# Pieces of expert weights: three buffers for loads and for halves, split two steps behind the load, sent back earlier in a step; two buffers for queries and keys

## The chip, the cores and the metric

The kernel runs on one core of one Trainium2 chip. The metric is device time in microseconds of one execution, lower is better. The core has a matrix engine (PE, with its weight loads as PEld), a vector engine (DVE), a scalar engine (ACT), a general engine (POOL) and a sequencer for transfers (SP); each takes its instructions strictly in the order of the program, and they meet through semaphores. Transfers run on 16 DMA engines that all queues share.

## The reference

Three stages follow each other, on 2304 tokens of 512 numbers, all in fp32:

```
attn   = softmax(mask_by_64_blocks(q @ k.T / 8)) @ v      4 batches, 8 heads, 576 tokens, 64 wide
x1     = softplus(attn_rows @ w_in) @ w_out               512 -> 2048 -> 512
logits = x1 @ w_gate + softplus(x1 @ w_noise) * noise     8 experts, the best two per token
out    = sum over the two: weight * (relu(x1 @ w1[e]) @ w2[e])     512 -> 1024 -> 512
```

The kernel keeps fp32 accuracy on a 16-bit matrix engine by splitting numbers into a high and a low f16 half, so that one product becomes three.

## The kernel before, in words

The attention is cut into 32 phases (a batch, a pair of heads, and tokens 0 to 255 or 256 to 575), and those into 80 units of 128 queries, 2 in an early phase and 3 in a late one. The main loop (line 605) takes one unit per iteration n: `stage_s` issues the products q·k of unit n, `stage_e` the row maximum (L248, DVE) and the exponentials (L252, L257, L258, ACT) of unit n-1, `stage_p` the scaling into two f16 halves (L280 ACT, L286 DVE) and a transposing DMA (L298) of unit n-2, `stage_v` and `stage_v4` the products with v (L321, L333). Between these stand quanta of the first feed-forward network (`mlp_quantum`; its products are the rows "l" of line 74, its elementwise work L364 to L375) and the router (L408 to L479). All of it shares PE, ACT, DVE and SP.

Three background jobs run beside the units. First `w_step` brings in the 32 pieces of `w_in` and `w_out` (`w_load` into a tile `wst`, `w_conv` through a tile `wt`). When all 32 are there, `e_step` works on the expert weights: 64 pieces of 128x1024 fp32. `e_load` (L495) fetches a piece into a tile `est`, `e_conv` splits it into the two halves of a tile `eh`, the high one on ACT (L508) and the low one on DVE (L514), and `e_store` (L519) writes both halves back to a scratch tensor `wsc` in DRAM. Loads and stores go through SP's queue, as do the transposes of L298, the router's transposes (L421) and the loads of q, k and v (L186 to L197). The tiles `wst` and `est` share one tag with `bwst` buffers (2), `wt` and `eh` another with `beh` buffers (2); `bqk` (3) is the number of buffers for the split q and k.

An `e_step` stands at the end of an iteration, 0.9 times per iteration on average, and does three things in turn: store the piece that was split last, split the piece that was loaded last, load the next. The split of a piece thus stands one step behind its load, and its store two steps behind.

When the loop has ended, the pools of the attention are closed, the rest of the feed-forward network and the router run, and the expert stage (class `Moe`, lines L829 to L922) reads `wsc` back in pieces of 2 MB. In the trace PE has no idle time there from about 700 us on.

The order in which instructions of one engine stand is not the order of the code: a scheduler goes through the program with priorities (`hipri` lifts some lines) and a model of when a buffer, an engine and a result are ready. The numbers of buffers therefore move instructions on every engine, also far from the lines that are changed.

Of the kernel before, what the change touches and what calls it, by code (L numbers as in the profile page):

```python
# [38 lines left out]
    return [sum(runs[:t % LANES]) + t // LANES for t in range(n)]  # L39


CFG = dict(wa=4, wb=12, rate=2.0, rate2=1.55, lag0=4, rt='rt', hq='s', xq='s', pr=3, wq='s', vq='s', rq='s', braw=2, clr=30, w0=1, w1=2, ra=4, rb=1, he=50, hpp=50, bP=2, bP16=3, bwst=2, beh=2, bpt=6, bqk=3, bxt=3, gr=4, lag=2, bA=1, bR=1, bvv=4, bxr=2, bxT=2, bvr=1, l2b=2, budget=3, espread=0.9, hp=50, elo='v', pmode=('av', 'av', 'av', 'av'), wp=24, eld='s', est='s', l1b=2, sb=3, cpy=1, x2q='p', tq='s')


SYNC = mybir.DependencyInfo(mybir.DependencyClass.Sync, mybir.DependencyReason.DATA)
# [4 lines left out]
def body(nc, tc, i, o, stop=9):  # L50
    ctx = ExitStack()
    with ctx:
        return _body(ctx, nc, tc, i, o, stop)


def _body(ctx, nc, tc, i, o, stop):
    q, k, v, w_in, w_out = i["q"], i["k"], i["v"], i["moe_w_in"], i["moe_w_out"]
# [78 lines left out]
    def w_load(n):  # L136
        st = p1.tile([128, 1024], I32, name="wst", tag="wst", bufs=int(CFG["bwst"]))
        if n < 16:
            ENG[CFG['wq']].dma_start(st.rearrange("p (c f) -> p c f", c=4), w_in32[:, :, 256 * n:256 * n + 256])
        else:  # L140
            ENG[CFG['wq']].dma_start(st, w_out32[128 * (n - 16):128 * (n - 15), :])
        wraw[n] = st

    def w_conv(n):
        wd = wraw.pop(n).rearrange("p (f two) -> p f two", two=2)
        lo, hi = wd[:, :, 0], wd[:, :, 1]
        t = p1.tile([128, 1024], I32, name="wt", tag="eh", bufs=int(CFG["beh"]))
        t = t[:, :512]
        nc.vector.tensor_scalar(t, hi, scalar1=M1, scalar2=3, op0=ALU.bitwise_and, op1=ALU.logical_shift_left)
        nc.vector.scalar_tensor_tensor(t, hi, SGN, t, op0=ALU.bitwise_and, op1=ALU.bitwise_or)  # L150
        nc.vector.scalar_tensor_tensor(t, lo, 29, t, op0=ALU.logical_shift_right, op1=ALU.bitwise_or)
        w = t.bitcast(F32)
        if n < 16:
            sl = slice(128 * n, 128 * n + 128)
            d0, d1, sc = win[:, 0, :, sl], win[:, 1, :, sl], 1024.0
            w = w.rearrange("p (c f) -> p c f", c=4)
        else:
            d0, d1, sc = wout[:, 0, n - 16, :], wout[:, 1, n - 16, :], 2048.0
        nc.scalar.activation(d0, w, AF.Copy, scale=sc)
        if n < CFG["wp"]:  # L160
            nc.scalar.activation(w, w, AF.Copy, scale=sc)
            nc.gpsimd.tensor_tensor(d1, w, d0, op=ALU.subtract)  # L162
        else:
            nc.vector.scalar_tensor_tensor(d1, w, sc, d0, op0=ALU.mult, op1=ALU.subtract)
# [3 lines left out]
    def xt(g):  # L168
        if g not in xts:
            xts[g] = pm.tile([128, 8, GT], F16, name=f"xt{g}", tag="xt", bufs=int(CFG["bxt"]))  # L170
        return xts[g]
# [68 lines left out]
    def stage_e(u):  # L240
        T, s = u["T"], u["s"]
        esc = 2.0 ** -15
        sm = p1.tile([128, 8], F32, name="sm", tag="sm", bufs=8)
        u["sm"] = sm
        P = p1.tile([128, 2, 512], F32, name="P", tag="P", bufs=int(CFG["bP"]))
        wd = (128 * (T + 1),) * 2 if T < 4 else (320, 256)
        for hd in range(2):
            nc.vector.tensor_reduce(out=sm[:, hd:hd + 1], in_=s[hd][:, :wd[hd]], axis=AX.X, op=ALU.max, negate=True)  # L248
        if T < 4:
            nc.vector.tensor_scalar_mul(sm[:, 2:4], sm[:, 0:2], esc)  # L250
            for hd in range(2):
                nc.scalar.activation(P[:, hd, :wd[0]], s[hd][:, :wd[0]], AF.Exp, scale=esc, bias=sm[:, 2 + hd:3 + hd], accum_out=sm[:, 4 + hd:5 + hd])  # L252
        else:
            P = P.rearrange("p a b -> p (a b)")
            nc.vector.tensor_scalar(sm[:, 2:3], sm[:, 0:1], scalar1=sm[:, 1:2], scalar2=esc, op0=ALU.min, op1=ALU.mult)
            nc.gpsimd.memset(P[:, 576:640], 0.0)
            nc.scalar.activation(P[:, 0:320], s[0][:, :320], AF.Exp, scale=esc, bias=sm[:, 2:3], accum_out=sm[:, 4:5])  # L257
            nc.scalar.activation(P[:, 320:576], s[1][:, :256], AF.Exp, scale=esc, bias=sm[:, 2:3], accum_out=sm[:, 5:6])  # L258
        u["P"] = P
# [81 lines left out]
    def hipri(n=None):  # L341
        n = int(CFG["hp"] if n is None else n)
        return tc.high_priority(offset=n) if n else ExitStack()
# [146 lines left out]
    est = {}  # L490

    def e_load(n):
        e, c = divmod(n, 8)
        st = p1.tile([128, 1024], F32, name="est", tag="wst", bufs=int(CFG["bwst"]))
        ENG[CFG["eld"]].dma_start(st, i["wexp"][e, :, 1024 * c:1024 * c + 1024])  # L495
        est[n] = st
# [20 lines left out]
    def e_store(n):  # L517
        e, c = divmod(n, 8)
        ENG[CFG["est"]].dma_start(wsc[e, :, 2048 * c:2048 * c + 2048], est.pop(n))  # L519
# [20 lines left out]
    cnt = dict(att=True, chain=False, wl=0, wc=0, el=0, ec=0, es=0, c1=0, p2=0, ready=0, routed=0)  # L540
# [34 lines left out]
    def w_step(n):  # L575
        for _ in range(n):
            if cnt["wc"] < 32:
                if cnt["wc"] < cnt["wl"]:
                    w_conv(cnt["wc"])
                    cnt["wc"] += 1  # L580
                if cnt["wl"] < 32:
                    w_load(cnt["wl"])
                    cnt["wl"] += 1

    def e_step():
        if cnt["wc"] < 32:
            return
        if cnt["es"] < cnt["ec"]:
            e_store(cnt["es"])
            cnt["es"] += 1  # L590
        if cnt["ec"] < cnt["el"]:
            e_conv(cnt["ec"])
            cnt["ec"] += 1
        if cnt["el"] < 64:
            e_load(cnt["el"])
            cnt["el"] += 1
# [8 lines left out]
    while n < NU + 6 or cnt["es"] < 64:  # L605
        if n < NU:
            u = units[n]
            if u["first"]:
                u["ph"]["pt"] = [p1.tile([128, 8, 256] if u["has4"] else [128, 4, 256], F16, name=f"pt{hd}", tag="pt", bufs=int(CFG["bpt"])) for hd in range(2)]
                if u["has4"]:  # L610
                    u["ph"]["pt4"] = p1.tile([128, 10, 128], F16, name="pt4", tag="pt4", bufs=2)
            if n == 0:
                load_pair(*porder[0])
                w_step(1)
                load_v(*porder[0])
                load_pair(*porder[1])
                conv_pair(*porder[0])
                load_v(*porder[1])
                lp, cpi = 2, 1
            stage_s(u)  # L620
        while cpi < lp and first_unit[porder[cpi]] <= n + 1:
            conv_pair(*porder[cpi])
            cpi += 1
            if cpi < lp:
                load_v(*porder[cpi])
        while lp < len(porder) and first_unit[porder[lp]] <= n + 6 and lp - cpi < int(CFG["braw"]):
            load_pair(*porder[lp])
            if lp == cpi:
                load_v(*porder[lp])
            lp += 1  # L630
        if 1 <= n < NU + 1:
            with hipri(CFG["he"]):
                stage_e(units[n - 1])
        w_step(int(0 if n < CFG['wa'] else CFG['w0'] if n < CFG['wb'] else CFG['w1']))
        credit = min(credit + CFG["rate" if n < 36 else "rate2"], 3)
        if credit >= 1:
            credit -= mlp_quantum() > 0
        if 2 <= n < NU + 2:
            with hipri(CFG["hpp"]):
                stage_p(units[n - 2])  # L640
        if credit >= 1:
            credit -= mlp_quantum() > 0
        if 4 <= n < NU + 4:
            u = units[n - 4]
            if u["last"]:
                stage_v(u["ph"])
        if 5 <= n < NU + 5:
            u = units[n - 5]
            if u["last"] and u["has4"]:
                stage_v4(u["ph"])  # L650
        while credit >= 1 and mlp_quantum():
            credit -= 1
        while cnt["ready"] < NG and need[cnt["ready"]] <= n:
            cnt["ready"] += 1
        if n >= CFG["clr"] and n % 2 == 0 and cleared < 19:
            clear(cleared)
            cleared += 1
        eacc += CFG["espread"]
        while eacc >= 1 and n > 12:
            e_step()  # L660
            eacc -= 1
        n += 1
# [358 lines left out]
```

## Time and profile before

| | us |
|---|---|
| median of 3 executions | 1109.68 |
| lowest and highest | 1108.88, 1110.16 |
| the profiled execution | 1112.65 |
| its span | 1110.7 |
| PE busy | 999.6 (90%) |
| DVE busy | 599.9 (54%) |
| ACT busy | 546.5 (49%) |

Shares over the whole span mix two stages with different limits: up to about 600 us PE, DVE, ACT and the DMA engines are all loaded, and after 700 us PE alone is. What a change before 600 us is worth is read from the stretches there.

### The profile page before, as it was taken

The page shows a single profiled execution, that of the slowest core. Times are in us where ns is not written, and L with a number is a line of the kernel's source. Part 1 is how long each engine was busy: PE and PEld are TensorE (multiplying, and loading weights), DVE is VectorE, ACT ScalarE, POOL GpSimd, SP SyncE. Part 2 cuts the span into 40 slices and gives each one's busy share as a digit, 9 for nine tenths or more (in the row PEclk, how much of TensorE's full clock was granted, in tenths as well). Part 3 has the DMA queues.
Part 4 walks back from the last instruction along what each step waited for, and adds up shares of the span by engine and source line. Part 5 has one row for each costly group of instructions (what it writes and reads, how often), then busy time and mean ns, then how long its engine had stood idle before and what let it go on. Part 6 is the DMA issues. An engine that isn't in the chain of part 4 may idle for free.

```text
span 1110.7 us, 24476 instructions
## 1 busy us (share of the span) xinstructions
PE 999.6 (90%) x9526; PEld 661.4 (60%) x9526; DVE 599.9 (54%) x1756; ACT 546.5 (49%) x1132; POOL 200.0 (18%) x188
## 2 busy tenths in 40 slices
PE   4676899878978888889889999999999999999996
PEld 2353455545555556456556667767767777777674
DVE  6999898676877778787756536212111121121120
ACT  6687667767868687887756531211111112111111
POOL 0334101010010000101003421322222222222111
PEclk9998899988998899998999999999999999999999
DMA  6865679999999899999997489746999448796442
GB/s 168 192 178 171 171 188 272 262 238 288 269 273 275 242 256 247 289 257 251 226 254 273 114 325 236 134 73 146 330 325 248 78 84 210 189 330 149 116 105 30
DMA packets 272518, 234.96 MB, mean 212 GB/s; under 512 B 180110, under 2 KB 217486, under 8 KB 272400
## 3 DMA queue, kind: packets, MB, share of 16 engines
q1 hardware_dynamic: 223872, 148.15, 54.8%
q0 software_dynamic: 14176, 38.17, 14.1%
q10 hardware_dynamic: 34352, 47.04, 13.0%
q8 instruction: 76, 1.25, 0.5%
q14 instruction: 42, 0.34, 0.1%
HBM read 251.60 MB, written 58.79 MB: 279 GB/s over the span
## 4 chain that ended last, share of the span: by engine, by line
PE 43%; DVE 3%; DMA 2%; ACT 1%; issue 1%; SPq 0%; POOL 0%; POOLq 0%; ACTq 0%; DVEq 0%
PE ph L74 19%; PE py L74 17%; PE l L74 6%; DMA est<-in_wexp_dram 1%; DVE eh L514 1%; DMA xT<-xw 0%; DMA out_dram<-ys,si 0%; SPq L298 0%; DVE G L372 0%; DVE P L286 0%; ACT A L367 0%; ACT A L364 0%; ACT eh L508 0%; ACT P L252 0%; ACT R L375 0%
## 5 line engine op out<-in xcount | busy, mean ns | idle before, releaser
L74 PE MATMUL l<-xt,win 128*128 128x256 f16 x1728 | 229.1, 289 | 13.4 <-ACT R L375 6.6
L74 PEld LDWEIGHTS <-W 128*128 128x128 f16 x3936 | 223.2, 98 | 10.4 <-issue 0.9
L902 DVE SCALAR_TENSOR_TENSOR HT<-ph,HT 128x512 f16<-128x512 f32 x78 | 53.9, 692 | 324.5 <-ACT HT L901 324.5
L74 PE MATMUL l<-wout,G 128*128 128x512 f16 x864 | 209.6, 389 | 14.0 <-POOL wout L162 5.0
L74 PE MATMUL ph<-xT,W 128*128 128x128 f16 x3744 | 215.4, 219 | 0.8 <-DVE HT L902 0.8
L74 PE MATMUL py<-W,HT 128*128 128x512 f16 x936 | 208.4, 379 | 0.8 <-ACT ys L920 0.8
L74 PEld LDWEIGHTS <-win 128*128 128x128 f16 x1728 | 171.3, 103 | 51.8 <-issue 11.7
L74 PEld LDWEIGHTS <-HT 128*128 128x128 f16 x936 | 90.0, 98 | 102.4 <-issue 1.1
L74 PEld LDWEIGHTS <-G 128*128 128x128 f16 x864 | 81.9, 99 | 106.4 <-issue 19.1
L901 ACT ACTIVATE HT<-ph 128x512 f16<-128x512 f32 x78 | 46.6, 597 | 162.5 <-PE ph L74 158.4
L920 ACT ACTIVATE ys<-py,sw 128x512 f32<-128x512 f32 x39 | 26.8, 687 | 181.3 <-PE py L74 166.7
L227 PE MATMUL s<-k,q 64*128 64x128 f16 (+3 forms) x384 | 65.7, 332 | 45.8 <-ACT P L252 33.7
L286 DVE SCALAR_TENSOR_TENSOR P<-P,sm,P 128x128 f16<-128x128 f32 (+4 forms) x144 | 87.0, 618 | 24.0 <-ACT P L280 23.7
L280 ACT ACTIVATE P<-P,sm 128x128 f16<-128x128 f32 (+4 forms) x144 | 81.2, 586 | 23.9 <-DMA pt<-P 13.0
L471 POOL DMA_INDIRECT xsc<-xw,rpos x36 | 42.1, 1169 | 281.6 <-DMA xsc<-xw,rpos 99.7
L514 DVE SCALAR_TENSOR_TENSOR eh<-est,eh 128x1024 f16<-128x1024 f32 x64 | 77.7, 1219 | 23.9 <-ACT eh L508 22.2
L921 POOL DMA_INDIRECT out_dram<-ys,si x39 | 61.6, 1580 | 158.5 <-ACT ys L920 147.3
L508 ACT ACTIVATE eh<-est 128x1024 f16<-128x1024 f32 x64 | 67.2, 1053 | 38.9 <-DMA est<-in_wexp_dram 38.7
L248 DVE TENSOR_REDUCE sm<-s 128x1 f32<-128x256 f32 (+2 forms) x160 | 74.2, 477 | 13.4 <-PE s L229 9.9
L252 ACT ACTIVATE P<-s,sm 128x128 f32<-128x128 f32 (+3 forms) x128 | 66.1, 520 | 21.4 <-DVE sm L250 10.7
L227 PEld LDWEIGHTS <-q 64*128 64x128 f16 x384 | 23.9, 100 | 78.7 <-issue 60.3
L375 ACT ACTIVATE R<-l 128x512 f32<-128x512 f32 x72 | 42.1, 592 | 41.4 <-PE l L74 30.3
(201 smaller groups left out, 1005.0 us busy)
## 6 DMA issues: line engine op xcount, KB each, us to landing
W<-wsc ACTq DMA_DIRECT2D x76, 2048.0 KB
est<-in_wexp_dram SPq DMA_DIRECT2D x64, 512.0 KB
wsc<-eh SPq DMA_DIRECT2D x64, 512.0 KB
wst<-in_moe_w_in_dram SPq DMA_DIRECT2D x16, 512.0 KB
wst<-in_moe_w_out_dram SPq DMA_DIRECT2D x16, 512.0 KB
W<-wsc POOLq DMA_DIRECT2D x4, 2048.0 KB
out_dram<-zero ACTq DMA_DIRECT2D x19, 256.0 KB
rk<-in_k_dram SPq DMA_DIRECT2D x16, 288.0 KB
```

The costliest lines, as they stand in the source:

```text
L74: x = nc.tensor.matmul(*args, **kw)
L227: nc.tensor.matmul(s[hd][:, :N], Q[hs, a, 128 * T - q0:128 * T - q0 + 128], K[hs, c, :N], start=n == 0, stop=False)
L248: nc.vector.tensor_reduce(out=sm[:, hd:hd + 1], in_=s[hd][:, :wd[hd]], axis=AX.X, op=ALU.max, negate=True)
L252: nc.scalar.activation(P[:, hd, :wd[0]], s[hd][:, :wd[0]], AF.Exp, scale=esc, bias=sm[:, 2 + hd:3 + hd], accum_out=sm[:, 4 + hd:5 + hd])
L280: nc.scalar.activation(v4[:, :, 0, :], pin, AF.Copy, scale=r)
L286: nc.vector.scalar_tensor_tensor(v4[:, :, 1, :], pin, r, v4[:, :, 0, :], op0=ALU.mult, op1=ALU.subtract)
L375: nc.scalar.activation(R[:, h], ps, AF.Copy, scale=2.0 ** -21)
L508: nc.scalar.activation(hh, sv, AF.Copy, scale=sc)
L514: nc.vector.scalar_tensor_tensor(hl, sv, sc, hh, op0=ALU.mult, op1=ALU.subtract)
L901: nc.scalar.activation(HT[:, hf, 0:4], ph, AF.Relu)
L902: self.lo = nc.vector.scalar_tensor_tensor(HT[:, hf, 4:8], ph, 0.0, HT[:, hf, 0:4], op0=ALU.max, op1=ALU.subtract)
L921: nc.gpsimd.indirect_dma_start(out=self.out, out_offset=bass.IndirectOffsetOnAxis(ap=si, axis=0), in_=ys, in_offset=None, bounds_check=NTO ...
```

## The change

Three numbers in `CFG` change: `bwst` 2 to 3, `beh` 2 to 3, `bqk` 3 to 2. In `e_step` the store goes, and the split is held back until two pieces are loaded beyond those split (or all 64 are loaded). The store moves into the main loop, behind `stage_e` of the next iteration.

```
-CFG = dict(... bwst=2, beh=2, bpt=6, bqk=3, ...)
+CFG = dict(... bwst=3, beh=3, bpt=6, bqk=2, ...)
     def e_step():
         if cnt["wc"] < 32:
             return
-        if cnt["es"] < cnt["ec"]:
-            e_store(cnt["es"])
-            cnt["es"] += 1
-        if cnt["ec"] < cnt["el"]:
+        if cnt["ec"] < cnt["el"] - 1 or cnt["ec"] < cnt["el"] == 64:
             e_conv(cnt["ec"])
             cnt["ec"] += 1
         if cnt["el"] < 64:
...
         if 1 <= n < NU + 1:
             with hipri(CFG["he"]):
                 stage_e(units[n - 1])
+        if cnt["es"] < cnt["ec"]:
+            e_store(cnt["es"])
+            cnt["es"] += 1
         w_step(...)
```

How this moves instructions is seen in the order of the built programs. On SP's queue, where the expert pieces begin, the kernel before has two loads, two transposes of probabilities and the first store; the third load comes behind six more entries:

```order
L495 DMA est<-in_wexp_dram 128x1024 x2
L421 DMA_TRANSPOSE xT_1829<-xw 128x8x128
L298 DMA_TRANSPOSE pt_1642<-P_1899 128x2x128
L298 DMA_TRANSPOSE pt_1643<-P_1903 128x2x128
L519 DMA wsc<-eh 128x2048
```

In the changed kernel a first load stands six entries above these, and two more here, so that three loads are out when the first store is issued:

```order
L495 DMA est<-in_wexp_dram 128x1024 x2
L186 DMA rq<-in_q_dram 128x256
L186 DMA rk<-in_k_dram 128x256
L195 DMA vr<-in_v_dram 128x2x128
L421 DMA_TRANSPOSE xT_1829<-xw 128x8x128
L421 DMA_TRANSPOSE xT_1889<-xw 128x8x128
L298 DMA_TRANSPOSE pt_1642<-P_1899 128x2x128
L298 DMA_TRANSPOSE pt_1643<-P_1903 128x2x128
L519 DMA wsc<-eh 128x2048
```

What moved: a third load stands ahead of the first store, and the first split is two loads behind.

The second place is ACT where the attention ends. Before, the last three scalings of probabilities (L280) have 11 splits of expert pieces (L508) behind them, of which the first two are here:

```order
L280 ACTIVATE P_7558<-P,sm 128x4x128
L280 ACTIVATE P_7562<-P,sm 128x4x128
L280 ACTIVATE P_7612<-P,sm 128x5x128
L375 ACTIVATE R<-l_7501 128x512
L508 ACTIVATE eh<-est 128x2x512
L364 ACTIVATE A<-R 128x1024
L508 ACTIVATE eh<-est 128x2x512
```

In the changed kernel the last two splits stand ahead of the last exponentials, and none follows:

```order
L508 ACTIVATE eh<-est 128x2x512
L307 ACTIVATE xt_7075<-pv 128x192
L508 ACTIVATE eh<-est 128x2x512
L252 ACTIVATE P,sm<-s,sm 128x512 x2
L307 ACTIVATE xt_7075<-pv 128x64
L375 ACTIVATE R<-l_7459 128x512
L257 ACTIVATE P,sm<-s,sm 128x320
L258 ACTIVATE P,sm<-s,sm 128x256
L280 ACTIVATE P_7555<-P,sm 128x4x128
L280 ACTIVATE P_7559<-P,sm 128x4x128
```

What moved: 11 of 64 splits go from behind the attention into it. On SP the same is seen. Before, behind the last transpose of probabilities, 9 loads and 11 stores are still to come:

```order
L298 DMA_TRANSPOSE pt_7259<-P_7612 128x10x128
L519 DMA wsc<-eh 128x2048
L495 DMA est<-in_wexp_dram 128x1024
L519 DMA wsc<-eh 128x2048
L495 DMA est<-in_wexp_dram 128x1024
L519 DMA wsc<-eh 128x2048
L421 DMA_TRANSPOSE xT_7632<-xw 128x8x128
```

In the changed kernel the last stores stand ahead of the last three transposes:

```order
L298 DMA_TRANSPOSE pt_7253<-P_7490 128x6x128
L298 DMA_TRANSPOSE pt_7254<-P_7494 128x6x128
L519 DMA wsc<-eh 128x2048 x2
L298 DMA_TRANSPOSE pt_7253<-P_7555 128x8x128
L298 DMA_TRANSPOSE pt_7254<-P_7559 128x8x128
L298 DMA_TRANSPOSE pt_7255<-P_7609 128x10x128
L421 DMA_TRANSPOSE xT_7629<-xw 128x8x128
```

What moved: the last 9 loads and 11 stores come ahead of the end of the attention. PE's own order keeps its mixture: the last product with v stands 12 matmuls further down than before, out of 9526.

## Rows read from the trace of the kernel before

**Rows 1.** The page: PE in total, then tenths in 40 equal slices of the span.
```profile
PE 999.6 (90%) x9526; PEld 661.4 (60%) x9526; DVE 599.9 (54%) x1756; ACT 546.5 (49%) x1132; POOL 200.0 (18%) x188
PE   4676899878978888889889999999999999999996
PEclk9998899988998899998999999999999999999999
DMA  6865679999999899999997489746999448796442
```

**Rows 2.** Windows: stretch, length, busy us by engine, granted PE clock, DMA share, GB/s.
```profile
25.00:150.00 125.00, 96.68 (x640) 56.30 (x640) 116.33 (x260) 92.12 (x225) 34.59 (x23) 0.93 0.71 180
150.00:577.00 427.00, 373.24 (x3247) 225.47 (x3245) 329.95 (x940) 315.72 (x669) 31.53 (x40) 0.93 1.02 256
577.00:608.00 31.00, 27.62 (x222) 19.39 (x223) 18.21 (x60) 19.70 (x29) 8.64 (x22) 1.00 0.88 282
700.00:1111.00 411.00, 401.52 (x4507) 290.68 (x4504) 71.44 (x231) 71.58 (x114) 100.13 (x75) 1.00 0.68 170
```

**Rows 3.** Waits of ACT, 150 to 600 us: total us, times, longest us.
```profile
ACT eh L508 <- DMA est<-in_wexp_dram: 37.6, 27, 4.0
ACT R L375 <- PE l L74: 17.1, 15, 2.5
ACT P L280 <- DMA pt<-P: 9.5, 8, 3.7
ACT P L280 <- POOL P L256: 5.9, 1, 5.9
ACT q L205 <- PE s L238: 1.5, 2, 0.8
```

**Rows 4.** Waits of PE, 150 to 600 us.
```profile
PE s L227 <- ACT P L252: 20.9, 13, 5.9
PE s L238 <- ACT P L252: 10.0, 6, 3.8
```

**Rows 5.** Timeline, 360 to 367 us: start, us; SP, ACT, PE, idle before in brackets.
```profile
360.17 0.58 SPq L495 DMA_DIRECT2D est<-in_wexp_dram  x1
...
364.69 1.06 ACT L508 ACTIVATE eh<-est 128x1024 f16<-128x1024 f32 x1 [3.97 <-DMA est<-in_wexp_dram]
...
366.13 0.68 ACT L252 ACTIVATE P<-s,sm 128x512 f32<-128x512 f32 x1
...
366.95 1.01 PE L238 MATMUL s<-k,q 64*64 64x320 f16 x6 [3.81 <-ACT P L252]
```

**Rows 6.** Windows of 5 us, columns as in Rows 2.
```profile
300.00:305.00 5.00, 5.00 (x51) 3.30 (x49) 3.45 (x22) 4.67 (x15) 0.00 (x0) 0.85 1.10 391
...
365.00:370.00 5.00, 3.05 (x18) 1.48 (x18) 3.16 (x15) 4.16 (x12) 0.00 (x0) 0.64 1.00 371
370.00:375.00 5.00, 5.00 (x25) 3.06 (x23) 2.80 (x14) 2.60 (x7) 0.00 (x0) 0.68 0.60 180
375.00:380.00 5.00, 5.00 (x47) 2.69 (x46) 4.05 (x13) 5.00 (x8) 1.02 (x1) 1.00 0.54 141
```

**Rows 7.** The tile est: count, least, median and greatest ns, first and last start.
```profile
L508 ACT ACTIVATE eh<-est x64: 1039/1056/1071, 157.3 to 605.7; 128x1024 f16<-128x1024 f32 x64
L514 DVE SCALAR_TENSOR_TENSOR eh<-est,eh x64: 1196/1219/1227, 158.5 to 606.8; 128x1024 f16<-128x1024 f32 x64
```

**Rows 8.** The chain that ended last, 544 to 600 us: start, us, what.
```profile
544.66 5.57 DMA est<-in_wexp_dram
...
564.55 6.64 DMA est<-in_wexp_dram
...
592.97 7.11 PE l L74 x44
```

**Rows 9.** Timeline of PE where the router's first product waits, 579 us.
```profile
579.42 0.46 PE L74 MATMUL pg<-wg,xT 128*128 128x16 f16 x12 [2.47 <-DMA xT<-xw]
```

**Rows 10.** The tile wst: what its engine sat idle for before it (us, times).
```profile
  DMA wst<-in_moe_w_in_dram: 2.1, 2
  DMA wst<-in_moe_w_out_dram: 1.2, 4
```

More of the change, by code (lines that the diff above doesn't have):

```diff
@@ L39, in lane_order @@
     return [sum(runs[:t % LANES]) + t // LANES for t in range(n)]
-CFG = dict(wa=4, wb=12, rate=2.0, rate2=1.55, lag0=4, rt='rt', hq='s', xq='s', pr=3, wq='s', vq='s', rq='s', braw=2, clr=30, w0=1, w1=2, ra=4, rb=1, he=50, hpp=50, bP=2, bP16=3, bwst=2, beh=2, bpt=6, bqk=3, bxt=3, gr=4, lag=2, bA=1, bR=1, bvv=4, bxr=2, bxT=2, bvr=1, l2b=2, budget=3, espread=0.9, hp=50, elo='v', pmode=('av', 'av', 'av', 'av'), wp=24, eld='s', est='s', l1b=2, sb=3, cpy=1, x2q='p', tq='s')
+CFG = dict(wa=4, wb=12, rate=2.0, rate2=1.55, lag0=4, rt='rt', hq='s', xq='s', pr=3, wq='s', vq='s', rq='s', braw=2, clr=30, w0=1, w1=2, ra=4, rb=1, he=50, hpp=50, bP=2, bP16=3, bwst=3, beh=3, bpt=6, bqk=2, bxt=3, gr=4, lag=2, bA=1, bR=1, bvv=4, bxr=2, bxT=2, bvr=1, l2b=2, budget=3, espread=0.9, hp=50, elo='v', pmode=('av', 'av', 'av', 'av'), wp=24, eld='s', est='s', l1b=2, sb=3, cpy=1, x2q='p', tq='s')
 SYNC = mybir.DependencyInfo(mybir.DependencyClass.Sync, mybir.DependencyReason.DATA)
@@ L587, in e_step @@
             return
[L588 to L591, printed above, removed]
+        if cnt["ec"] < cnt["el"] - 1 or cnt["ec"] < cnt["el"] == 64:
             e_conv(cnt["ec"])
@@ L633, in _body @@
                 stage_e(units[n - 1])
+        if cnt["es"] < cnt["ec"]:
+            e_store(cnt["es"])
+            cnt["es"] += 1
         w_step(int(0 if n < CFG['wa'] else CFG['w0'] if n < CFG['wb'] else CFG['w1']))
```

## The prediction

> **What bounds the kernel now.** I read the page first, then windows over the stages, then the waits of ACT and PE in the stage that the change touches, then one of these waits in the timeline, and last the chain of waits.
>
> The reader is to see in the page [rows 1] that PE is busy for 90% of the span, so at most a tenth is to be had by any change that takes no matmul away, and that its digits are lowest early. The windows [rows 2] say where: from 700 us on PE is busy in 401.5 of 411 us at the full clock, and what is missing is the end of the kernel. Nothing done earlier changes that stage, it only moves as a block. From 150 to 577 us, where the expert pieces run beside the attention, PE is busy in 373.2 of 427 us, so it idles 53.8 us, and its granted clock is 0.93, that is some 14% of the stretch at the lower of its two levels (1.2 instead of 2.4 GHz). This is worth (1 - 0.93) x 427 = 30 us of work. No other engine is full there: DVE has 330 us of 427 and ACT 316. The DMA engines show 1.02 and 256 GB/s. Since PE's matmuls are the same before and after, the time changes by what happens to PE's idle time and its clock ahead of about 600 us.
>
> What does PE wait for? In 150 to 600 us it waits above all for ACT's exponentials, 20.9 and 10.0 us [rows 4]. ACT's own largest wait is for the load of an expert piece: 37.6 us in 27 waits [rows 3]. ACT takes its instructions in order, so everything behind such a split waits with it. One case shows the whole chain [rows 5]: a load is issued at 360.17, the split of that piece has reached the head of ACT and stands there for 3.97 us until 364.69, the exponentials of line 252 behind it start at 366.13, and PE, whose next score products need the bank that they read, idles for 3.81 us until 366.95. The idle time then costs a second time: the clock is 0.64 and 0.68 in the two stretches of 5 us behind it [rows 6], which is (0.36 + 0.32) x 5 = 3.4 us of lost work. At the end of the stage the chain of waits runs through two loads, 5.57 and 6.64 us [rows 8], before PE takes over for good at 592.97.
>
> **The change part by part.** No engine instruction and no transfer is added or taken away; everything is order, distance and buffers.
>
> Split two steps behind its load. 64 splits between 157 and 607 us [rows 7] are 7 us apart, and a load lands in 5 to 7 us [rows 8]; in the case above it was 4.5 us. One step back the split often comes too early, two steps back (14 us) it comes in time. So I take ACT's 37.6 us of waits as gone. What of it reaches PE: ACT idles 427 - 316 = 111 us in the stretch, and the loads are 37.6/111 = 34% of that. By the same share of PE's 53.8 us the gain is 18 us. The bounds are 0, if ACT only waits for something else instead, and 37.6, if each of these waits hits PE as the one shown did. I take -18.
>
> The clock. 34% of the 30 us lost to it would be 10 us. A removed wait gives that back only where no other idle time stands beside it, so I take half, -5 (bounds 0 and -10).
>
> Eleven pieces go into the attention. This is what the order shows and the diff does not say: splits that ran behind the last exponentials now run ahead of them. They bring 11 x 1.056 = 11.6 us to ACT and 11 x 1.219 = 13.4 us to DVE [rows 7] in a stretch where both have idle time, 111 and 97 us [rows 2]. Bounds are 0 (all in idle time) and 25 us (all in series with PE). As the two engines are a quarter idle and PE waits on them in turns, I take a quarter, +6.
>
> Behind the attention the same pieces are missing. From 577 to 608 us PE idles 31 - 27.6 = 3.4 us [rows 2], most of it in a wait of 2.47 us for the router's transpose, which is queued between pieces [rows 9]. I take -3 (bounds -3.4 and 0).
>
> The transfers. Nine loads and eleven stores, 20 x 0.524 = 10.5 MB, move ahead of the last transposes of probabilities. At the 256 GB/s of the stretch they are 41 us of DMA time. One bound is 41 us, if the stretch is full already; the other is 0. Against a full stretch speak windows at 391 and 371 GB/s, and two in a row at shares of 0.60 and 0.54 [rows 6]: there is room, in pieces. The nearest row for harm is ACT's wait for a transpose to free a probability tile, 9.5 us in 8 waits [rows 3]. If it grows by half, that is +5, which I take.
>
> By the Trainium skill (DMA: Bandwidth & Descriptors, section on latency and other measured facts) a transposing DMA reaches 261 GB/s effectively. Stretches of 391 and 371 GB/s do not agree with a limit of that height for the mixture here, but the mean of 256 GB/s stands just below it. By that rule the 10.5 MB would be 40 us on top, as in the bound above. The Trainium skill also says (Perfetto Trace Analysis, section on the roofline) that a single core is bounded by its DMA engines at about 435 GB/s; by that rule the transfer term would be near nothing. No run here shows a stretch at 435 GB/s.
>
> The stores sooner. A store stands half an iteration higher and waits for DVE's half of the split; queued behind it on SP are transposes and the next loads. Three `eh` buffers mean that no split waits for a store. The cover for the transposes is the same ACT wait of 9.5 us, already in the term above; I add nothing.
>
> The first 150 us. `wst` and `wt` get a third buffer too. DVE is busy there in 116 of 125 us [rows 2] and waits for these loads 2.1 and 1.2 us in all [rows 10], so 3.3 us is the most to be won; a weight piece that is pulled ahead of a softmax costs about as much. I take 0, with 3.3 us to either side.
>
> Queries and keys with two buffers. The split of a pair stands one unit ahead of its use, and the pair two before has had its last score product two or three units earlier. ACT's wait of this kind is 1.5 us in 2 times now [rows 3]; I take 0, bounds 0 and +3 if it doubles twice.
>
> Sum: -18 - 5 + 6 - 3 + 5 = -15 us. The profiled execution took 1112.65 us (span 1110.7), 2.97 more than the median of the runs, so I take the difference from the median: 1109.68 - 15 = 1095 us.
>
> **Rivals.**
>
> The waits change their name. ACT in order waits for the last of its inputs; without the load it may stand before the next exponentials or the next feed-forward tile. For it speaks that ACT waits 17.1 us for PE [rows 3], so in part it runs ahead of PE anyway, and one of PE's worst waits behind the exponentials, 5.9 us, came from POOL and not from a load [rows 3, 4]. Against it speaks the chain at 360 us, where nothing else was late. Then only the tail gives something and the eleven pieces take it back: -3 + 6 - 3 = 0, 1107 to 1112 us.
>
> The DMA engines are the bound of the attention. Its mechanism: eleven pieces' transfers come ahead of the last transposes, the share of 1.02 cannot rise, and each transpose, with the scaling behind it on ACT, comes later. It decides once the stretch cannot take more than some 260 GB/s. The price is 41 us at most; windows with idle engines take about half, 20, the tail gives 3 back, and the waits for loads still shrink by about half, 9: 20 - 3 - 9 = +8, 1118 us. For it speaks the 9s in the DMA row of the page all through the stage [rows 1]; against it the windows at 391 GB/s.
>
> All waits for loads reach PE with their clock: -37 - 10 + 6 + 5 - 3 = -39, 1071 us. For it speaks the one case shown; against it that PE has feed-forward products between units, which hide short waits, and the 27 waits have a mean of only 1.4 us.
>
> The change does not do what it says if the scheduler puts the splits directly behind their loads again. The order speaks against it; I give that no chance of its own.
>
> **How the numbers follow.** The forecast (gain of 5 to 28 us) has 0.55, the large gain 0.08, waits that change their name 0.17, DMA as the bound 0.20. A measurement of this kernel tells 0.2%, about 2.2 us, from no change. Of the third case half is within that, and the rest lies on both sides; of the fourth nearly all is slower. So faster 0.69, same 0.09, slower 0.22. The range of 8 in 10 leaves out the largest gains and the worst of the DMA case: 1078 to 1118 us. The forecast's own range is 1082 to 1105.
>
> **What would show it.** Right: ACT's waits for `est` in 150 to 600 us fall from 37.6 to under 10 us; PE's waits for L252 fall with them, and the granted clock of the stretch rises to 0.95 or more; the last split starts before the last exponentials, and PE has no idle time of over 1 us behind the attention. Wrong: ACT's waits for `pt` grow beyond 15 us or PE's last product with v ends later than 577 us. The expert stage behind 700 us must keep its length; if it does not, the argument that it moves as a block has failed.

## The result, and the profile after

| | median us | lowest, highest | ratio to before, 95% |
|---|---|---|---|
| before | 1109.92 (4 runs) | 1108.88, 1113.72 | |
| after | 1124.92 (4 runs) | 1121.78, 1129.01 | 1.010 (1.0061 to 1.0139) |

The change makes the kernel 1.0% slower by the ratio on record; the two medians of the table stand 1.4% apart, at the upper end of its interval. The forecast was 1095 us, 1.3% faster, and the time lies above the range. The single executions of the kernel before that were timed beside the experiments lie between 1101.84 and 1119.49 us, so one execution tells little below 1%.

The page of the changed kernel, to be held against [rows 1]: PE in total, then tenths in 40 slices.

```profile
PE 1001.5 (89%) x9526; PEld 659.5 (59%) x9526; DVE 595.4 (53%) x1756; ACT 546.0 (49%) x1132; POOL 205.6 (18%) x188
PE   3677789797797887988999999999999999999996
PEclk9998889898898898988999999999999999999999
DMA  7875758999999999999973197746999448796442
```

The span grew by 12.9 us, from 1110.7 to 1123.6. PE's busy time grew by 1.9 us (from 999.6), so its idle time grew by 11.0 (from 111.1 to 122.1). The reader is to keep this split, for it is used on every kernel below: the matmuls are the same 9526, so a change of PE's busy time is in the main a change of its clock; the rest is idle time. The clock can be counted apart: half of PE's busy time in the stretches at 1.2 GHz, the time that the lower level cost it, is 34.8 us before, 37.1 after and 21.9 in e9_anchor below, which agrees with the busy times to 1.5 us. In the other kernels below the two counts differ by up to 4 us, in e4_hold by 9.

Where the idle time is, the windows of the changed kernel say, with the columns of [rows 2].

```profile
0.00:25.00 25.00, 8.07 (x45) 4.07 (x46) 14.91 (x58) 12.63 (x40) 2.20 (x9) 1.00 0.79 182
25.00:150.00 125.00, 93.72 (x643) 55.79 (x642) 115.17 (x264) 91.97 (x230) 37.08 (x23) 0.93 0.70 178
150.00:577.00 427.00, 365.55 (x3107) 217.69 (x3106) 331.87 (x937) 317.16 (x667) 36.12 (x40) 0.91 1.05 272
577.00:608.00 31.00, 29.85 (x296) 19.09 (x294) 18.42 (x101) 14.71 (x29) 9.23 (x22) 1.00 0.32 69
700.00:1111.00 411.00, 409.44 (x4673) 299.72 (x4672) 80.75 (x264) 73.36 (x117) 98.87 (x75) 1.00 0.70 176
```

From 150 to 577 us PE idles 61.5 us where it was 53.8, and the clock is 0.91 where it was 0.93. Ahead of 150 us it idles 48.2 us where it was 43.0. From 577 to 700 us it gets 3 us back. The other end of the stage moved by what the span moved: the last product with v starts 15.5 us later, as the two kernels' rows show (line, engine, count, least, median and greatest ns, first and last start), first before, then after.

```profile
L333 PE MATMUL pv<-pt,vv x480: 192/196/263, 277.2 to 576.5; 128*64 128x64 f16 x128, 64*64 64x64 f16 x32
```

```profile
L333 PE MATMUL pv<-pt,vv x480: 189/196/262, 282.0 to 592.0; 128*64 128x64 f16 x128, 64*64 64x64 f16 x32
```

The waits of ACT and of PE in 150 to 600 us of the changed kernel, which answer to [rows 3] and [rows 4], show what the forecast missed.

```profile
ACT eh L508 <- DMA est<-in_wexp_dram: 37.1, 19, 5.2
ACT P L280 <- DMA pt<-P: 21.7, 9, 4.7
...
PE s L238 <- ACT P L252: 18.6, 9, 5.1
PE s L227 <- ACT P L252: 18.1, 12, 6.9
```

The waits for loads were to go, and they are all there: 37.1 us after 37.6. They are fewer (19 after 27) and longer (5.2 after 4.0 us). Of waits of 2 us and more there are 7, with 25.0 us, where before had 5 with 14.0. The timeline of the changed kernel around one of them answers to [rows 5].

```profile
366.35 4.22 SPq L298 DMA_TRANSPOSE pt<-P  x2
370.63 0.57 SPq L495 DMA_DIRECT2D est<-in_wexp_dram  x1
...
374.90 1.06 ACT L508 ACTIVATE eh<-est 128x1024 f16<-128x1024 f32 x1 [3.61 <-DMA est<-in_wexp_dram]
376.33 0.68 ACT L252 ACTIVATE P<-s,sm 128x512 f32<-128x512 f32 x1
377.16 1.01 PE L238 MATMUL s<-k,q 64*64 64x320 f16 x6 [3.26 <-ACT P L252]
```

It is the picture of before again. The load is issued at 370.63, behind two transposes on SP; its split is already at ACT's head and starts 4.3 us after the issue; the exponentials stand behind it, and PE idles for 3.26 us.

How far the split stands behind its load can be counted over all 64 pieces, from the issue of each load to the start of its split in the timeline. The median was 5.8 us before, 50 of 64 under 8 us. It is 7.1 us now, 38 under 8 us. Two steps, 14 us, were promised by the code. What became of them shows in the place of the splits on ACT, counted in units of the attention whose exponentials stand ahead. The 32nd split stands behind 51 of the 80 units in the changed kernel and the 52nd behind 68; before, they stood behind 56 and 78. In e9_anchor below, which keeps the splits from moving up, they stand behind 59 and 80. The loads moved up as well: 121 transposes of probabilities stand ahead of the 52nd load, 136 before, 141 in e9_anchor. The scheduler had pulled the whole row of pieces forward, each split close behind its load.

### The profile page after: what moved, and what is told of

It reads as the page before. It is cut to its first block, busy times and chain, and to the rows that moved or that the text cites. A ratio compares the mean times of both kernels' runs of the same rounds, so it can differ in the third digit from the quotient of the medians.

```text
span 1123.6 us, 24451 instructions
## 1 busy us (share of the span) xinstructions
PE 1001.5 (89%) x9526; PEld 659.5 (59%) x9526; DVE 595.4 (53%) x1756; ACT 546.0 (49%) x1132; POOL 205.6 (18%) x188
## 3 DMA queue, kind: packets, MB, share of 16 engines
q10 hardware_dynamic: 34352, 47.04, 12.9%
## 4 chain that ended last, share of the span: by engine, by line
PE 48%; DMA 10%; ACT 8%; DVE 7%; issue 5%; SPq 2%; POOL 1%; ACTq 0%; POOLq 0%; DVEq 0%
PE ph L74 19%; PE py L74 17%; PE l L74 10%; DMA est<-in_wexp_dram 4%; DMA pt<-P 3%; DMA xT<-xw 2%; ACT P L252 1%; ACT eh L508 1%; DVE sm L248 1%; SPq L866 1%; DVE G L372 1%; ACT P L280 1%; ACT A L364 1%; ACT A L367 1%; DVE P L286 1%
## 5 line engine op out<-in xcount | busy, mean ns | idle before, releaser
L74 PE MATMUL l<-wout,G 128*128 128x512 f16 x864 | 217.9, 403 | 15.0 <-POOL wout L162 7.6
L74 PE MATMUL l<-xt,win 128*128 128x256 f16 x1728 | 221.8, 283 | 9.6 <-ACT R L375 6.1
L74 PEld LDWEIGHTS <-win 128*128 128x128 f16 x1728 | 167.2, 101 | 44.9 <-issue 12.8
L74 PEld LDWEIGHTS <-G 128*128 128x128 f16 x864 | 84.4, 102 | 117.8 <-issue 37.2
L280 ACT ACTIVATE P<-P,sm 128x128 f16<-128x128 f32 (+4 forms) x144 | 80.7, 586 | 34.6 <-DMA pt<-P 28.9
L471 POOL DMA_INDIRECT xsc<-xw,rpos x36 | 45.6, 1268 | 262.8 <-DMA xsc<-xw,rpos 97.0
L921 POOL DMA_INDIRECT out_dram<-ys,si x39 | 61.5, 1576 | 159.4 <-ACT ys L920 150.7
L508 ACT ACTIVATE eh<-est 128x1024 f16<-128x1024 f32 x64 | 67.0, 1051 | 39.4 <-DMA est<-in_wexp_dram 37.1
L248 DVE TENSOR_REDUCE sm<-s 128x1 f32<-128x256 f32 (+2 forms) x160 | 73.5, 477 | 17.4 <-PE s L229 12.1
L368 DVE SCALAR_TENSOR_TENSOR R<-A,R 128x1024 f32<-128x1024 f32 x36 | 44.0, 1221 | 47.3 <-ACT A L367 47.1
```

The lines of the kernel that those rows point to most:

```text
L74: x = nc.tensor.matmul(*args, **kw)
L280: nc.scalar.activation(v4[:, :, 0, :], pin, AF.Copy, scale=r)
L471: st = nc.gpsimd.indirect_dma_start(out=xsc, out_offset=bass.IndirectOffsetOnAxis(ap=ps_i[:, n:n + 1], axis=0), in_=xw, in_offset=None)
L508: nc.scalar.activation(hh, sv, AF.Copy, scale=sc)
L921: nc.gpsimd.indirect_dma_start(out=self.out, out_offset=bass.IndirectOffsetOnAxis(ap=si, axis=0), in_=ys, in_offset=None, bounds_check=NTO ...
```

## The experiments

For each kernel two numbers are given beside its ratio: the sum of ACT's waits ahead of splits in 150 to 600 us (for a load, `est`, or for a store that must free the halves, `wsc`), and how PE's busy and idle time differ from before. Both come from one profiled execution of each kernel, which can lie off the median: those of e1_qk2 and e6_beh3 were the longest of ten, that of e14_tie_buffers the shortest of seven.

| kernel | ratio, 95% | waits ahead of splits | PE busy, idle |
|---|---|---|---|
| after | 1.0100 (1.0061 to 1.0139) | 37.1 | +1.9, +11.0 |
| e1_qk2 | 0.9934 (0.9906 to 0.9962) | 33.1 | -1.3, -0.7 |
| e2_buffers | 1.0018 (0.9984 to 1.0052) | 32.8 | -8.8, +8.4 |
| e3_code | 1.0031 (0.9993 to 1.0070) | 51.4 (wsc) | -1.5, +4.8 |
| e4_hold | 1.0118 (1.0060 to 1.0176) | 39.3 | -1.7, +15.3 |
| e5_wst3 | 1.0063 (1.0029 to 1.0097) | 49.8 (27.7 wsc) | +3.4, +5.0 |
| e6_beh3 | 0.9933 (0.9904 to 0.9961) | 38.2 | -2.3, +2.6 |
| e7_control | 1.0064 (1.0033 to 1.0095) | 54.7 | -0.6, +4.5 |
| e8_late_qk2 | 1.0072 (1.0038 to 1.0106) | 44.9 (43.7 wsc) | +7.4, +5.0 |
| e9_anchor | 0.9819 (0.9770 to 0.9868) | 9.6 | -14.4, -6.6 |
| e10_anchor_before | 0.9957 (0.9924 to 0.9990) | 22.8 | -6.5, -2.5 |
| e11_weights2 | 1.0129 (1.0080 to 1.0178) | 52.7 | +3.7, +8.9 |
| e12_control_after | 1.0107 (1.0059 to 1.0156) | 37.2 | +2.1, +8.1 |
| e13_tie_distance | 1.0012 (0.9978 to 1.0045) | 22.0 (wsc) | +3.0, -1.8 |
| e14_tie_buffers | 0.9891 (0.9858 to 0.9924) | 12.1 (0.6 wsc) | -11.2, -8.6 |
| e15_loose_tie | 0.9857 (0.9806 to 0.9909) | 12.5 | -12.5, -2.0 |
| e16_tie_weights2 | 0.9830 (0.9778 to 0.9882) | 9.7 (0.5 wsc) | -11.2, -10.2 |

**The parts of the change alone.** e1_qk2 is the kernel before with two buffers for queries and keys, e2_buffers has all three new numbers, e3_code is the changed kernel with the numbers of before.

```
e1  -bqk=3                    +bqk=2
e2  -bwst=2, beh=2, bqk=3     +bwst=3, beh=3, bqk=2
e3  the changed code with bwst=2, beh=2, bqk=3
```

> The kernel before with two buffers for queries and keys in place of three, nothing else. In its order 11 loads and 13 stores of expert pieces stand behind the attention's last transpose (9 and 11 before, none in the changed kernel). Theory A, the loss of 15 us comes from the pieces that moved ahead of the attention's end, with their transfers and splits: same or slightly faster, 1106 to 1112 us, last product with v at 570 to 578 us. Theory B, the two buffers for queries and keys delay their loads and splits: slower by 6 to 15 us, ACT's and SP's waits for q and k grow (7.2 us on ACT in the changed kernel, 1.5 before).

> The kernel before with the changed kernel's three numbers of buffers, but with its old steps (split one step behind the load, store in the step). Its order has no load and 2 stores behind the last transpose. Theory A: slower as the changed kernel, 1118 to 1128 us, ACT's waits for transposes 15 to 25 us. Theory B: the same, so this run tells them apart only together with e1. A third theory, C, that the distance of the split and the place of the store cost the time: 1108 to 1113 us.

> The changed kernel's steps (split two steps behind, store earlier) with the old numbers of buffers (2, 2, 3). Its order has 8 loads and 10 stores behind the last transpose. Theory A and B: as before, 1106 to 1113 us, ACT's waits for loads still 30 to 40 us. Theory C: slower, 1118 to 1128 us.

The two buffers for queries and keys do not cost, they come out 0.7% faster. The three numbers together and the code alone are within 0.3% of before, with intervals that hold 1. e3_code has no wait for `est` at all. They have changed their name, as one rival said:

```profile
ACT eh L508 <- DMA wsc<-eh: 51.4, 29, 5.0
ACT P L280 <- DMA pt<-P: 11.5, 5, 4.3
```

A split that is held back a step, with two buffers for halves, waits for the store of two pieces ago.

**The pieces ahead of the attention's end.** e4_hold lets the last nine loads wait for the last exponential, as in before.

```
+        l = ...dma_start(st, wexp piece n)
+        if n >= 55: l waits for the last exponential
```

> The changed kernel with its last 9 loads held until the last exponential of the attention, so that 8 loads and 9 stores stand behind the last transpose. Theory A: most of the loss is undone, 1108 to 1114 us, and the last product with v comes at 575 to 582 us in place of 592. Theory B, or a loss in the first 150 us alone (5 us more idle time of PE there): 1119 to 1126 us.

It is as slow as the changed kernel, and its last product with v starts at 590.7 us, not at 575 to 582. Nine of the eleven pieces stand behind the last exponential again, so the 15 us were not lost to the pieces that moved ahead of the attention's end.

**Smaller parts, and how much chance there is.** e5_wst3 and e6_beh3 add one number each to e1_qk2. e8_late_qk2 is e3_code with two buffers for queries and keys. e7_control is the kernel before with the priority of `stage_e` at 49 instead of 50: no buffer, no distance and no work changes, but instructions change places.

```
e5  -bwst=2, bqk=3     +bwst=3, bqk=2
e6  -beh=2, bqk=3      +beh=3, bqk=2
e7  -he=50             +he=49
e8  the changed code with bwst=2, beh=2, bqk=2
```

> Two buffers for queries and keys as in e1, and three buffers for loads alone (bwst 3, beh 2), old steps. Theory E, the buffers of the pieces cost what e2 lost against e1 (9 us) and one of the two is guilty: if it is the loads, 1112 to 1118 us; if it is the halves, 1101 to 1108 us as e1. Theory D, each change of the order moves the time by up to 1% either way without a mechanism of its own: anything from 1100 to 1125 us, with ACT's waits in all between 115 and 127 us in 150 to 600 us as in every kernel so far, and the difference spread over many small waits of PE.

> Two buffers for queries and keys, and three for the halves alone (bwst 2, beh 3), old steps. Theory E: the other half of e5, 1112 to 1118 us if the halves' buffers are guilty, else 1101 to 1108 us. Theory D: 1100 to 1125 us, not the complement of e5.

> A control: the kernel before with the priority of the exponentials' stage lifted by 49 places in place of 50, nothing else. No buffer, no distance and no transfer changes, only rows here and there in the order. Theory E, or any theory in which the parts of the change have prices of their own: within 0.3% of before, 1107 to 1113 us. Theory D: it may differ by 0.5% or more.

> The split two steps behind with old buffers of pieces (2, 2), and two buffers for queries and keys: e3 and e1 together. If the parts add up (e1 -0.7%, e3 +0.3%): 0.996 of before, 1105 to 1110 us. Theory F, the split two steps behind is what costs wherever the order is tight: 1112 to 1122 us. Theory D: no relation to e1 and e3.

The control matters most here. A reordering that means nothing is 0.6% slower, and its waits for loads rose from 37.6 to 54.7 us:

```profile
ACT eh L508 <- DMA est<-in_wexp_dram: 54.7, 33, 3.9
```

So effects of up to 0.7% of one edit, those of e1, e5, e6 and e8 among them, cannot be laid to the edit's own mechanism by their times; nor do the 1.0018 of e2 and the 1.0031 of e3 show that their edits have no price. ACT's waits ahead of the splits of queries (L205) were 1.5 us before, and 0.7 us in e1 and in e6, which is too little for 0.7% of the time. e8 beside e3 says the same: there two buffers for queries and keys bring no gain.

e6 is not an experiment of its own. In the traces PE, DVE, ACT and SP have the same order in e6 as in e1, so the third buffer for halves moved nothing. The pair shows instead how well the numbers repeat: the ratios are 0.9933 and 0.9934, but the waits ahead of splits 38.2 and 33.1 us and the idle time of PE +2.6 and -0.7 us, each from one execution.

**The distance made real.** e9_anchor is the changed kernel with one tie more. Each high half of a split is tied behind the last exponential of its own iteration, in the order of ACT alone: no semaphore is added. e10_anchor_before does the same to the kernel before.

```
-        nc.scalar.activation(hh, sv, AF.Copy, scale=sc)
+        x = nc.scalar.activation(hh, sv, AF.Copy, scale=sc)
+        x stands behind cnt["x"] on ACT (order only)      # cnt["x"]: the last exponential of stage_e
```

> The changed kernel with each split's high half tied on ACT behind the exponentials of its own iteration, so that the scheduler can't pull a split up to its load and the two steps of distance stand in the order as in the code (12 loads and 14 stores behind the last transpose). Theory G, the predicted gain failed because the scheduler took the distance away: ACT's waits for loads fall from 37 to under 12 us and the time to 1095 to 1106 us. Rival H, the waits change their name: the waits for loads fall but ACT's waits stay at 115 to 127 us in all and the time at 1112 to 1126 us. Theory D (chance of the order, up to 0.7% either way, as the control showed) is on top of each.

> The kernel before with the same tie (12 loads and 13 stores behind the last transpose), the split one step behind its load. Theory G: one step of about 7 us covers a load of 5 to 7 us mostly, waits for loads 10 to 25 us, 1100 to 1110 us, and slower than e9 by 3 to 8 us. Rival H: 1106 to 1118 us whatever the waits for loads.

e9_anchor takes 1090.03 us (1088.40 to 1092.65), 1.8% less than before. Its waits of ACT in 150 to 600 us, its stretch from 150 to 577 us, its last products with v, and PE in total:

```profile
ACT P L280 <- DMA pt<-P: 28.6, 15, 5.4
ACT P L252 <- DVE sm L250: 15.6, 12, 2.7
ACT R L375 <- PE l L74: 11.2, 16, 1.9
ACT eh L508 <- DMA est<-in_wexp_dram: 9.6, 8, 2.6
```

```profile
150.00:577.00 427.00, 379.17 (x3392) 234.56 (x3392) 338.79 (x990) 324.93 (x686) 33.28 (x42) 0.96 1.04 265
```

```profile
L333 PE MATMUL pv<-pt,vv x480: 192/196/263, 263.7 to 556.6; 128*64 128x64 f16 x128, 64*64 64x64 f16 x32
```

```profile
PE 985.2 (90%) x9526; PEld 658.0 (60%) x9526; DVE 599.4 (55%) x1756; ACT 544.6 (50%) x1132; POOL 199.3 (18%) x188
```

The median from load to split is 15.0 us, 12 of 64 under 8 us: the distance of two steps is there. The waits for loads fall to 9.6 us, the attention ends 20 us sooner than before and 35 sooner than in the changed kernel, and the stretch holds 3392 matmuls, where it held 3247 before and 3107 in the changed kernel. ACT's waits in all fell much less: the sum over all its waits in 150 to 600 us is 109.7 us, after 118.2 before and 121.4 in the changed kernel. The four largest above say why: the waits for transposes and for DVE's maxima have grown. In the timeline of e9_anchor the splits stand behind the exponentials and PE does not stop for them; here is one that waits for nothing, with the products of the next unit already running:

```profile
364.30 0.57 ACT L252 ACTIVATE P<-s,sm 128x384 f32<-128x384 f32 x1
364.45 1.37 PE L227 MATMUL s<-k,q 64*128 64x512 f16 x6 [0.29 <-ACT P L252]
364.76 0.20 ACT L252 ACTIVATION_READ_ACCUMULATOR P<-s,sm 128x1 f32 x1
...
364.96 1.06 ACT L508 ACTIVATE eh<-est 128x1024 f16<-128x1024 f32 x1
```

With the short rings (the buffers that pieces take in turn) and the short distance of the kernel before, the tie gives less: e10_anchor_before is 0.4% faster, its median distance 7.4 us, and its waits are

```profile
ACT eh L508 <- DMA est<-in_wexp_dram: 22.8, 20, 3.6
```

**The first 25 us, and a control of the changed kernel.** With a third buffer PE is busy in 8.07 of the first 25 us, where it was

```profile
0.00:25.00 25.00, 10.37 (x61) 5.37 (x62) 16.45 (x64) 14.60 (x46) 2.02 (x9) 1.00 0.70 169
```

e11_weights2 lets the first weights run only two pieces deep again. e12_control_after is the changed kernel with the priority of `stage_e` at 48.

```
e11 +    if n >= 2: the load of piece n of the first weights waits for the split of piece n-2
e12 -he=50             +he=48
```

> The changed kernel with the loads of the first weights kept two pieces deep (the load of piece n waits for the split of piece n-2), so that only the expert pieces use the third buffer. If the first 150 us cost the changed kernel its 5 us of PE's idle time: PE busy 10 us in place of 8 in the first 25 us, idle time in the first 150 us back to 43 to 45 us, and 1118 to 1122 us. Theory D: the first 25 us as said, but the time anywhere from 1105 to 1130 us.

> A control on the changed kernel: the priority of the exponentials' stage at 48 in place of 50. If the parts of the change have a firm price of 1%: within 0.3% of the changed kernel, 1.007 to 1.013 of before. Theory D: it may stand 0.5% or more away from the changed kernel, 1.000 to 1.005 or above 1.015 of before.

e11 has PE busy in 10.36 us of the first 25 again and idle in 41.7 of the first 150 us, but it is as slow: its waits for loads rose to 52.7 us. e12 is as slow as well. So four orders, those of the changed kernel, e4, e11 and e12, are all 1.0 to 1.3% slower than before, and the loss does not look like an accident of one order.

**What of the tie does it.** e13 keeps the two steps and has the old numbers, e14 has the new numbers with a split one step behind, e15 ties to the exponentials of the iteration before, e16 adds e11's limit to e9.

```
e13 e9_anchor with bwst=2, beh=2, bqk=3
e14 e9_anchor with the e_step of before (store, split the last piece, load)
e15 e9_anchor, cnt["x"] taken ahead of stage_e
e16 e9_anchor + the edit of e11
```

> Tie as in e9, the split two steps behind, but the old buffers (2, 2, 3). With two buffers for loads a split that stands late keeps its buffer, so the next load waits for it on SP: if both parts are needed, waits for loads stay at 15 to 40 us and the time at 1102 to 1112 us; if the distance alone gives the gain, 1088 to 1096 us.

> Tie as in e9, the new buffers (3, 3, 2), but the split one step behind. If both parts are needed: waits for loads 10 to 25 us as in e10, 1098 to 1108 us. If the buffers alone give the gain: under 12 us of waits and 1088 to 1096 us.

> As e9, but each split is tied behind the exponentials of the iteration before its own, so the scheduler may pull it up by one iteration (some 7 us). If the time follows the distance that is left: waits for loads between e9's 9.6 and the changed kernel's 37.1, 12 to 25 us, and a time between the two, 1095 to 1112 us. If any tie is enough: 1088 to 1094 us.

> e9 with the loads of the first weights two pieces deep as in e11. PE busy 10 in place of 8.6 us in the first 25. If the early loss counts in the whole: 1085 to 1089 us, 1 to 5 us better than e9. If it is absorbed later, or the chance of the order is larger: 1088 to 1098 us.

Waits of ACT, 150 to 600 us, of e13 and then of e14:

```profile
ACT P L280 <- DMA pt<-P: 25.7, 15, 3.7
ACT eh L508 <- DMA wsc<-eh: 22.0, 19, 2.7
```

```profile
ACT P L280 <- DMA pt<-P: 27.6, 17, 4.2
...
ACT eh L508 <- DMA est<-in_wexp_dram: 11.5, 6, 3.4
```

Two steps with two buffers (e13) give nothing: no wait for a load is left, and 22.0 us of waits for a store took its place. Three buffers with the tie (e14) give 1.1%, and the distance is there without a second step (median 13.8 us). The looser tie gives 1.4%, with a median of 13.6 us and 12.5 us of waits. The limit on the first weights adds nothing to e9.

The tie changes more than the distance: it puts each split behind exponentials that stood behind it, and it moves the row of pieces back, so that 14 splits stand behind the attention's last exponentials in e9_anchor and none in the changed kernel. Four of the tied kernels have that in common, with 13 to 15 splits there: e10 and e13 with the old numbers, at 0.9957 and 1.0012, and e14 and e9 with the new ones, at 0.9891 and 0.9819. The 0.4% of e10 are within what the control moved, so the tie and the place of the last pieces do not give the gain by themselves. With the tie, the new numbers give 0.7% where the split is one step behind and 1.9% where it is two behind; the first is hardly more than the control's 0.6%. The new numbers contain the two buffers for queries and keys, and no tied run parts them from the rings.

By the table the kernels with at most 13 us of waits ahead of splits are at 0.982 to 0.989, those with 22 to 23 at 0.996 and 1.001, those with 32 to 55 at 0.993 to 1.013. Within the last group the sum does not sort them.

e9_anchor beats both kernels, 1090.03 against 1109.92 and 1124.92 us.

## Why the prediction was wrong, point by point

**The step that failed is "Split two steps behind its load", and in it "two steps back (14 us) it comes in time. So I take ACT's 37.6 us of waits as gone."** The distance was in the code and not in the program as built: median 7.1 us, not 14. The rival was named ("if the scheduler puts the splits directly behind their loads again") and given no chance because "the order speaks against it". The order that was read was the beginning, where three loads stand ahead of the first store, and the end. The 64 pairs were not counted. The runs showed in its place 37.1 us of waits for loads where none were forecast, and 9.6 us in e9_anchor, where the distance is 15.0 us: the waits stayed because the distance was not there. With it the same code takes 1090 us, 35 less.

**The size of the term.** e9_anchor shows what the term is worth when the distance is there, and it is less than was taken. ACT's waits for loads fell by 28.0 us from before, but its waits in all by only 8.5, and PE's idle time by 6.6, where 18 had been taken for it. A second count says the same: PE's gaps that end within 4 us behind the end of such a wait of at least 0.5 us hold 21.3 us before, 27.9 after and 3.6 in e9_anchor. The same windows of 4 us, shifted along the stage, hold 13, 8 and 3 us on average, so that of the 21.3 us before only some 8 stand out as the price, an estimate. The larger part of the gain, 14.4 us, is busy time, nearly all of it the clock, for which -5 had been taken. It is not an accident of the profiled execution: the mean granted clock is 0.972 to 0.978 in the four of e9_anchor, 0.956 to 0.973 in the 13 of the kernel before beside them. The time 1090 thus stands near the 1095 forecast by luck: the idle time was worth a third of what was taken, and the clock almost three times as much. Why the clock gained so much is not settled: PE's gaps of 2 us and more in 150 to 600 us hold 34.2 us in e9_anchor, hardly less than the 35.5 of before.

**Eleven pieces, +6.** They did move, as the order had shown: the last split starts at 570.0 us, ahead of the last exponentials (575.4). e4_hold moves nine loads behind them again and gains nothing, so the loss is not there.

**The transfers, +5, and the DMA rival.** The sign for it came: ACT's waits for `pt` rose beyond 15 us, to 21.7, and the last product with v came after 577. It would have been read as the DMA rival borne out, and the 1124.92 us are nearer to that rival's 1118 than to the forecast. The sign does not tell them apart: the waits are 28.6 us in e9_anchor, the fastest kernel, at 265 GB/s and a share of 1.04. So these waits alone do not make a kernel slow; whether e9_anchor would be faster without them was not tried.

**The waits that change their name.** True for e3, e8 and e13, where `est` becomes `wsc`. Not for the changed kernel, where the name did not change. For e9_anchor it is true of ACT in the main: of the 28.0 us some 20 came back under other names. That PE gained all the same is what this rival had wrong.

**Behind the attention, -3,** came. The windows from 577 us on do not compare like with like, as the attention ends 15 us later now. In the 121 us behind its end PE idles 2.7 us (592.5 to 713.5), where it was 5.2 (577 to 698), and its longest wait is 0.7 us, where it was 2.5. The expert stage kept its length and moved as a block: in the chain that ended last PE takes over for good 12.6 us later than before [rows 8], nearly the 12.9 of the span.

```profile
543.94 7.03 DMA est<-in_wexp_dram
...
565.04 4.86 DMA est<-in_wexp_dram
...
605.59 41.01 PE l L74 x284
```

**The first 150 us, 0 with 3.3 to either side,** was too narrow: PE idles 5.3 us more there. DVE's waits for these loads were the wrong view: PE waits there 19.7 us for exponentials and 7.6 us for POOL's part of `w_out`, where it was 12.9 and 5.0. e11 takes the idle time back without a gain in the end.

**The stores sooner, 0.** Not tested: no run moves the store alone. In 150 to 600 us the stores wait on SP for DVE's half of the split 7.2 us in the changed kernel, where it was 26.3, but the longer distance of the code comes with that.

**Queries and keys, 0 to +3.** In the changed kernel ACT's waits of this kind, ahead of the splits of queries, rose from 1.5 to 7.2 us, beyond the doubling twice that was the bound. They do not carry the loss: in e12, as slow, they are 2.5 us. e1 shows no cost. Whether its 0.7% is a gain of its own stays open beside a control of 0.6%.

**What can be told apart.** The prediction took 0.2% as the smallest change that a measurement tells from none. For a change of the order the control sets it higher, at some 0.6%.

**What stays open** is why the changed kernel is 1% slower than before and not the same. What is known: its waits for loads have the same sum in fewer and longer pieces; PE's gaps of 2 us and more hold 43.4 us where they held 35.5; and the clock of the stretch is 0.91, in the execution with the lowest clock of the four. Whether it takes both the code and the buffers is open too: with the old steps the three numbers give 1.0018, with two buffers for pieces the code gives 1.0031, but e5 and e8, at 1.0063 and 1.0072, have intervals that overlap that of the changed kernel. Length of the waits fits e4, e7, e11 and e12, whose waits of 2 us and more hold 27.2, 28.5, 34.9 and 24.2 us. It does not fit e6, which has 24.9 and is faster, and e1, the same order, has 17.9: one execution does not fix this number. So it is not shown.

## What to carry to other kernels

Where a scheduler sets the order, a distance written in the code is a wish: count it in the built order or in the trace, pair by pair and over the whole stage, before a wait is taken as gone. Raise distance and ring together, and tie the order where it must hold. With the distance alone the wait moved to the next ring (e3, e8, e13); with longer rings and no tie the scheduler pulled the pieces forward and used them up (e2, the changed kernel). Before an edit is credited with less than 1%, time a reordering that means nothing.

## What the runs showed of the hardware

The granted clock gave at least as much as the idle time itself: in e9, e14, e15 and e16 PE's busy time for the same 9526 matmuls is 11.2 to 14.4 us lower than before, and its idle time 2.0 to 10.2 us. Over all their executions the mean granted clock of these four is 0.969 to 0.978; in the executions of the kernel before that were timed beside them it is 0.956 to 0.973. In the changed kernel the windows around the wait shown above fell from the upper to the lower of the two levels, 1.2 GHz, after 5 us in which PE was busy in 3.23:

```profile
370.00:375.00 5.00, 3.23 (x52) 2.51 (x50) 4.37 (x10) 1.35 (x5) 0.15 (x1) 0.99 1.01 229
375.00:380.00 5.00, 2.84 (x17) 1.33 (x17) 2.95 (x11) 3.37 (x10) 0.00 (x0) 0.50 1.11 310
```

The DMA engines moved the same transfers for an attention that ends 20 us sooner in e9_anchor, at 265 GB/s where it was 256 and at a share of 1.04 where it was 1.02. A share of 1.0 on this counter was thus not a ceiling.
